# Moving q, k and x across partitions by DMA so that attention runs on 64x64 tiles: one change to a fused attention and feed-forward kernel

## The chip, the cores and the metric

The kernel runs on one core of one Trainium2 chip. The metric is the time of one execution on the device, in microseconds (us). The profiler's span of a run is about 1.8 us shorter than its time. Where not said otherwise, all quoted times are medians of fast executions; an execution is called slow when it took over 1.5 % longer than the fastest of its kernel. PE is the matrix engine (TensorE), DVE is VectorE, ACT is ScalarE, POOL is GpSimd and SP is SyncE, which here only issues DMAs.

## The reference

Attention inside chunks of 64 tokens, then a feed-forward block in which two products are multiplied:

```python
# q, k, v: (8, 8, 576, 64) = batch, heads, tokens, head dim; chunk = 64
scores = scale * np.matmul(q_c, k_c.transpose(0, 1, 2, 4, 3))
scores = scores - np.max(scores, axis=-1, keepdims=True)
attn = np.exp(scores)
attn = attn / (np.sum(attn, axis=-1, keepdims=True) + 1e-09)
out = np.matmul(attn, v_c)
# ... heads joined: x is (4608, 512)
a = x @ w1            # w1, w2: (512, 1024)
b = x @ w2
h = a * b @ w3        # w3: (1024, 1024)
return (h @ w_out).astype(np.float32)     # w_out: (1024, 512)
```

The tokens are worked off as 18 "pairs" of 256 tokens (four chunks). The kernel multiplies w3 and w_out once into one matrix `w3o`.

## The kernel before

A string gives the order in which steps are emitted, each a letter and a pair: `l` loads q, k, v; `T` transposes q and k within blocks of 32 partitions (DVE); `S` scores (PE); `E` exponentials (ACT); `P` values (PE); `N` division (DVE); `X` transposes x (DVE); `A` and `B` the products a and b in four parts (PE); `C` copies a out of PSUM (ACT); `M` multiplies it by b (DVE); `O` the output product (PE); `Y` copies it (ACT) and issues its DMA (SP). Each engine takes its steps strictly in this order. All PSUM results share one pool of four tiles of 2 x 512 f32 in each partition.

```python
ps = ctx.enter_context(tc.tile_pool(name="ps", bufs=4, space=bass.MemoryType.PSUM))

def do_T(p, s):
    if s == 0:
        qkT_t[p] = asb.tile([P, 2, 2, H, CH], bf, tag="qkT", bufs=2, name="qkT")
    inorder(nc.vector.transpose(...))          # cut

def do_S(p):                                   # 8 x 2 x 4 = 64 products, contraction over 32
    qkT = qkT_t.pop(p)
    s_t[p] = psum("s_ps")
    for h in range(H):
        for e in range(2):
            for i in range(NB):
                mm(s_t[p][half[i % 2], i // 2, h * CH:(h + 1) * CH],
                   lhsT=qkT[blk[i], 1, e, h, :],
                   rhs=qkT[blk[i], 0, e, h, :], start=(e == 0), stop=(e == 1))
# do_P: 2 x 2 x 2 x 4 x 2 = 64 products, e[half, ..., 32 columns] by vbuf[half]     (cut)

def do_C(p, j):
    a_t[p, j] = msb.tile([P, 512], f32, tag="a_sb", bufs=3, name="a_sb")
    inorder(nc.scalar.copy(a_t[p, j][:], ps_t[p, j][:, 0, :]))
# do_M: ab = a_sb * ps_t[p, j][:, 1, :], which frees the PSUM tile of A and B        (cut)

def do_Y(p):                                   # last pair: in two halves (cut)
    inorder(nc.scalar.copy(o_sb[:, u0:u1], t[:, u0:u1]))
    inorder(nc.sync.dma_start(
        out[p * PT + u0 * UT:p * PT + u1 * UT].rearrange("(u p) n -> p u n", p=UT), o_sb[:, u0:u1]))
```

The softmax here doesn't subtract the row's maximum and nothing guards it: scores larger than these inputs give would overflow.

## Time and profile before

| | |
|---|---|
| time | 262.31 us, median of 3 (262.27 to 262.46) |
| PE busy | 89 % of the span |
| mean granted PE clock | 0.986 of full speed |
| two pairs in the steady part | 24.0 us (158.1 to 182.1), two output products among them |

From the page of the kernel before: the busy time of each engine, and three rows that cut the span into 40 slices of 6.5 us (busy tenths of PE, tenths of the granted clock, and the mean busy share of the 16 DMA engines).

```profile
PE 231.9 (89%) x3796; PEld 169.8 (65%) x3808; DVE 153.7 (59%) x231; ACT 84.1 (32%) x114; POOL 84.5 (32%) x112
PE   0259948999999698999899999999999999999992
PEclk9999995999999999999999999999999999999999
DMA  7999999999999999929931004002200220220344
```

PE starts late, has some gaps while the loads come in (the DMA row stands at 7 and then at 9 for the first 17 slices, 110 us), and from then on is full to the end. DMA is nearly idle in the second half: it looks as if it could take on work for nothing.

The timeline of PE in the kernel before, a stretch of two pairs. Columns: start, length, engine, line, operation, output and inputs, tile and shapes, count; in brackets idle time before it and what ended it.

```profile
158.12 7.15 PE L88 MATMUL ab_ps<-xt,w 128*128 128x256 bf16 x64
165.20 0.70 PE L88 MATMUL pv<-vbuf,e 64*32 64x65 bf16 x64
165.83 0.71 PE L88 MATMUL s_ps<-qkT 32*64 32x64 bf16 x64
166.66 7.15 PE L88 MATMUL ab_ps<-xt,w 128*128 128x256 bf16 x64
...
175.21 7.07 PE L88 MATMUL o_ps<-w3o,ab 128*128 128x512 bf16 x31
182.11 0.27 PE L88 MATMUL ab_ps<-xt,w 128*128 128x256 bf16 x1
```

Start to start, the values (`pv`) take 0.63 us and the scores (`s_ps`) 0.83 us of every pair. No bracket stands on any of these lines: PE waits for nothing.

All DMA instructions on `out_dram` in the kernel before (nanoseconds, min/median/max), and their time from issue to landing:

```profile
L249 SPq DMA_DIRECT2D out_dram<-o_sb x19: 344/372/429, 107.0 to 256.8; - x19
DMA to landing us min/median/max: 2.0/2.8/4.7
```

SP has 19 DMAs in the whole kernel. The issue of one takes it 0.37 us.

### The profile page before, as it was taken

How to read it: one execution, taken by the hardware profiler on the slowest of the kernel's cores; microseconds unless marked ns; L12 is line 12 of the kernel's file. 1: busy time of each engine (PE TensorE's matmuls, PEld its weight loads, DVE VectorE, ACT ScalarE, POOL GpSimd, SP SyncE). 2: the span in 40 equal slices, each digit the busy share in tenths (PEclk: the TensorE clock that was granted, in tenths of full speed). 3: DMA queues.
4: the chain of work that ended last, by engine and by line, in shares of the span. 5: the costliest groups of instructions: out<-in, count | busy, mean ns of one | idle time of the engine just before them, and what ended most of it. 6: DMA issues, size and time to landing. Idle time of an engine off the chain costs nothing.

```text
span 260.2 us, 8288 instructions
## 1 busy us (share of the span) xinstructions
PE 231.9 (89%) x3796; PEld 169.8 (65%) x3808; DVE 153.7 (59%) x231; ACT 84.1 (32%) x114; POOL 84.5 (32%) x112
## 2 busy tenths in 40 slices
PE   0259948999999698999899999999999999999992
PEld 0248836875686586588568857884886588484440
DVE  1676685799989869539824982697276047121000
ACT  1112430324433243333233343432443333242331
POOL 8956854778975996105200000000000000000000
PEclk9999995999999999999999999999999999999999
DMA  7999999999999999929931004002200220220344
GB/s 78 168 196 178 179 200 196 187 170 170 171 170 173 161 173 173 196 83 93 75 103 62 3 4 161 5 3 80 84 3 3 83 83 0 77 86 27 135 164 161
DMA packets 89619, 29.38 MB, mean 113 GB/s; under 512 B 75760, under 2 KB 84976, under 8 KB 89584
## 3 DMA queue, kind: packets, MB, share of 16 engines
q0 software_dynamic: 84672, 19.41, 80.1%
...
## 4 chain that ended last, share of the span: by engine, by line
PE 65%; DMA 14%; POOL 8%; DVE 6%; issue 3%; ACT 2%; ACTq 0%; POOLq 0%
PE ab_ps L88 35%; PE o_ps L88 24%; DMA w<-in_moe_w_dram 8%; PE w_ps L88 4%; DMA wo<-in_moe_w_out_dram 4%; DVE ab L232 3%; POOL qk L91 3%; POOL vbuf L91 3%; DMA qk<-in_k_dram 2%; ACT a_sb L227 2%; POOL w L91 2%; DVE qkT L159 1%; PE pv L88 1%; PE s_ps L88 1%; POOL wo L91 1%
## 5 line engine op out<-in xcount | busy, mean ns | idle before, releaser
L88 PE MATMUL ab_ps<-xt,w 128*128 128x256 bf16 x1152 | 132.6, 277 | 3.0 <-issue 2.2
L88 PEld LDWEIGHTS <-w 128*128 128x128 bf16 x1152 | 114.0, 99 | 19.9 <-issue 2.6
L232 DVE TENSOR_TENSOR ab<-a_sb,ab_ps 128x512 bf16<-128x512 f32 x72 | 48.6, 676 | 69.5 <-ACT a_sb L227 69.5
L227 ACT COPY a_sb<-ab_ps 128x512 f32<-128x512 f32 x72 | 42.1, 585 | 92.9 <-PE ab_ps L88 87.1
L88 PE MATMUL o_ps<-w3o,ab 128*128 128x512 bf16 x280 | 62.9, 379 | 1.4 <-DVE ab L232 0.6
L88 PEld LDWEIGHTS <-ab 128*128 128x128 bf16 x288 | 28.1, 98 | 33.5 <-issue 0.6
L159 DVE STREAM_TRANSPOSE qkT<-qk 128x1024 bf16<-128x1024 bf16 x36 | 45.7, 1292 | 6.6 <-DMA qk<-in_q_dram 6.5
...
L248 ACT COPY o_sb<-o_ps 128x1024 f32<-128x1024 f32 (+1 forms) x19 | 18.3, 967 | 46.4 <-PE o_ps L88 46.4
L204 DVE STREAM_TRANSPOSE xt<-xn 128x512 bf16<-128x512 bf16 x36 | 25.5, 709 | 1.1
L200 DVE TENSOR_TENSOR xn<-pv,rc 128x512 bf16<-128x512 f32 x36 | 24.9, 691 | 1.2
L175 ACT ACTIVATE e<-s_ps 128x1024 bf16<-128x1024 f32 x18 | 18.4, 1023 | 22.1 <-PE s_ps L88 22.1
L88 PE MATMUL s_ps<-qkT 32*64 32x64 bf16 x1152 | 13.6, 198 | 11.7 <-DVE qkT L159 10.8
...
L88 PEld LDWEIGHTS <-qkT 32*64 32x64 bf16 x1152 | 11.5, 110 | 13.3 <-DVE qkT L159 10.9
L88 PE MATMUL pv<-vbuf,e 64*32 64x65 bf16 x1152 | 13.0, 201 | 7.4 <-issue 4.0
L88 PEld LDWEIGHTS <-e 64*32 64x32 bf16 x1152 | 10.1, 91 | 11.8 <-issue 7.6
L88 PE MATMUL w_ps<-wo,w3T 128*128 128x512 bf16 x60 | 14.3, 379 | 0.2
L91 POOL DMA_DIRECT2D w<-in_moe_w_dram x16 | 11.1, 694 | 6.4 <-DMA wo<-in_moe_w_out_dram 2.8
L88 PEld LDWEIGHTS <-w3T 128*128 128x128 bf16 x64 | 6.1, 98 | 6.7
L256 DVE STREAM_TRANSPOSE w3T<-w 128x1024 bf16<-128x1024 bf16 x8 | 9.6, 1213 | 0.0
(9 smaller groups left out, 15.1 us busy)
## 6 DMA issues: line engine op xcount, KB each, us to landing
...
```

The costliest lines, as they stand in the source:

```text
L88: return inorder(nc.tensor.matmul(*a, **kw))
L91: return inorder(nc.gpsimd.dma_start(dst, src))
L159: inorder(nc.vector.transpose(qkT_t[p][:, s].rearrange("p e h (y t) -> p h t e y", t=2), qk_t[p][:, s].rearrange("p h (t e y) -> p h t e y ...
L175: inorder(nc.scalar.activation(e_t[p][:].rearrange("p u h q -> p u (h q)"), s_t.pop(p)[:], Exp, scale=scale, bias=0.0))
L200: inorder(nc.vector.tensor_mul(xn_t[p, u][:], pv[:, :, :, 0:D], rc.to_broadcast([P, 2, 4, D])))
L204: inorder(nc.vector.transpose(xt[:, :, t0:t0 + UT].rearrange("p o (m y) -> p m o y", y=BL), xn_t.pop((p, u))[:].rearrange("p r (c n) (z o) ...
L227: inorder(nc.scalar.copy(a_t[p, j][:], ps_t[p, j][:, 0, :]))
L232: inorder(nc.vector.tensor_mul(ab_t[p][:, 2 * j:2 * j + 2, :].rearrange("p j t -> p (j t)"), a_t.pop((p, j))[:], ps_t.pop((p, j))[:, 1, :]))
L248: inorder(nc.scalar.copy(o_sb[:, u0:u1], t[:, u0:u1]))
L256: inorder(nc.vector.transpose(w3T_t[f][:].rearrange("p k (f y) -> p f k y", y=BL), w3[:, NB * f:NB * (f + 1), :].rearrange("p f (k x) -> p ...
```

## The change

The intent: from pair 4 on, let DMA bring the two 32-row parts of each contraction into one 64-row half of the array, so that scores and values need 32 products each on 64x64 tiles and not 64 each on 32x64 and 64x32 tiles. `G` moves q and k, `H` moves x back; each is eight DMAs of 32 partitions, SBUF to SBUF, on SP. The new layout permutes the tokens of a pair, so an output is now a DMA whose DRAM side is written `(c y) n` with c = 4. Besides, the first quarter of w1, w2 is loaded behind pair 0, the order is retuned, and the last output is cut in three. Core of the diff (the order string, renamed views and warm-up products on zeros are cut):

```diff
+    def move(dst, src):
+        inorder(nc.sync.dma_start(dst, src))
+    def do_G(p):
+        qkT = qkT_t.pop(p)
+        qkm_t[p] = asb.tile([P, 2, 2, H, CH], bf, tag="qkm", bufs=2, name="qkm")
+        for i in range(NB):
+            for e in range(2):
+                move(qkm_t[p][blk[i // 2 * 2 + e], i % 2], qkT[blk[i], e])
 ... do_S, p >= 4
+            for h in range(H):
+                for i in (0, 3, 1, 2):
+                    mm(s_t[p][half[i % 2], i // 2, h * CH:(h + 1) * CH],
+                       lhsT=qkm[half[i // 2], i % 2, 1, h, :], rhs=qkm[half[i // 2], i % 2, 0, h, :],
+                       start=True, stop=True)
 ... do_P, p >= 4
+                    for g, r in ((0, 0), (1, 1), (1, 0), (0, 1)):
+                        mm(pv[half[g], r, m * W:(m + 1) * W], lhsT=e[half[r], u, 4 * g + m, :],
+                           rhs=vbuf[p % 7][half[r], u, 4 * g + m, 0:W], start=True, stop=True)
+    def do_H(p):
+        for k_ in range(2):
+            for i in range(NB):
+                move(xt[blk[i // 2 * 2 + k_], p, i % 2], xm_t[p][blk[i], k_])
 ... outputs
+    def out_rows(p, u):
+        return out[p * PT:(p + 1) * PT].rearrange("(c u y) n -> u c y n", u=2, y=BL)[u]
+        for u in range(2):
+            move(out_rows(p, u), o_sb[:, u])
```

More of the change, by code (lines that the diff above doesn't have):

```diff
@@ L9 @@
 ORDER = """
-l0 l1 i0 i1 i2 l2 i3 l3 o h0 h1 l4 l5 T0.0 T0.1 l6 S0 E0 T1.0 P0 N0.0 T1.1 l7 X0.0 S1 N0.1 E1 X0.1
-P1 A0.0 N1.0 X1.0 N1.1 B0.0 C0.0 X1.1 A1.0 M0.0 B1.0 C1.0 A0.1 M1.0 B0.1 T2.0 C0.1 A1.1 M0.1 B1.1
-T2.1 l8 C1.1 A0.2 M1.1 B0.2 C0.2 A1.2 M0.2 B1.2 C1.2 A0.3 M1.2 B0.3 C0.3 T3.0 S2 A1.3 M0.3 E2 T3.1
-B1.3 C1.3 P2 l9 M1.3 S3 N2.0 E3 X2.0 N2.1 P3 X2.1 N3.0 A2.0 X3.0 B2.0 C2.0 N3.1 A2.1 M2.0 B2.1 X3.1
-C2.1 A2.2 M2.1 B2.2 C2.2 A2.3 M2.2 B2.3 V0 C2.3 A3.0 M2.3 B3.0 V1 C3.0 A3.1 M3.0 B3.1 V2 C3.1 A3.2
@@ L15 @@
-M3.1 B3.2 C3.2 V3 A3.3 M3.2 B3.3 C3.3 T4.0 W0 M3.3 T4.1 l10 S4 T5.0 Z0 W1 E4 V4 T5.1 V5 P4 l11 Z1 V6
-S5 W2 E5 N4.0 X4.0 N4.1 X4.1 V7 A4.0 Z2 T6.0 B4.0 C4.0 A4.1 T6.1 B4.1 C4.1 M4.0 A4.2 M4.1 B4.2 T7.0
-C4.2 P5 l12 M4.2 S6 N5.0 A4.3 E6 X5.0 B4.3 N5.1 C4.3 W3 X5.1 M4.3 T7.1 T8.0 P6 l13 Z3 T8.1 S7 A5.0
-N6.0 E7 X6.0 B5.0 C5.0 N6.1 A5.1 M5.0 B5.1 X6.1 C5.1 T9.0 A5.2 B5.2 C5.2 M5.1 T9.1 A5.3 B5.3 C5.3
-M5.2 A6.0 M5.3 B6.0 C6.0 P7 l14 M6.0 S8 N7.0 A6.1 E8 X7.0 N7.1 B6.1 C6.1 X7.1 A6.2 M6.1 B6.2 C6.2
@@ L20 @@
-T10.0 A6.3 M6.2 B6.3 C6.3 T10.1 P8 l15 S9 M6.3 N8.0 O0 E9 X8.0 N8.1 X8.1 T11.0 O1 Y0 T11.1 A7.0 Y1
-B7.0 C7.0 A7.1 M7.0 B7.1 C7.1 A7.2 M7.1 B7.2 C7.2 A7.3 M7.2 B7.3 C7.3 P9 l16 M7.3 S10 N9.0 A8.0 E10
-X9.0 N9.1 B8.0 C8.0 X9.1 A8.1 M8.0 B8.1 C8.1 T12.0 A8.2 M8.1 B8.2 C8.2 T12.1 A8.3 M8.2 B8.3 C8.3 P10
-l17 M8.3 S11 N10.0 O2 E11 X10.0 N10.1 X10.1 T13.0 O3 T13.1 Y2 A9.0 Y3 B9.0 C9.0 A9.1 M9.0 B9.1 C9.1
-A9.2 M9.1 B9.2 C9.2 A9.3 M9.2 B9.3 C9.3 P11 M9.3 S12 N11.0 A10.0 E12 X11.0 N11.1 B10.0 C10.0 X11.1
@@ L25 @@
-A10.1 M10.0 B10.1 C10.1 T14.0 A10.2 M10.1 B10.2 C10.2 T14.1 A10.3 M10.2 B10.3 C10.3 P12 M10.3 S13
-N12.0 O4 E13 X12.0 N12.1 X12.1 T15.0 O5 T15.1 Y4 A11.0 Y5 B11.0 C11.0 A11.1 M11.0 B11.1 C11.1 A11.2
-M11.1 B11.2 C11.2 A11.3 M11.2 B11.3 C11.3 P13 M11.3 S14 N13.0 A12.0 E14 X13.0 N13.1 B12.0 C12.0
-X13.1 A12.1 M12.0 B12.1 C12.1 T16.0 A12.2 M12.1 B12.2 C12.2 T16.1 A12.3 M12.2 B12.3 C12.3 P14 M12.3
-S15 N14.0 O6 E15 X14.0 N14.1 X14.1 T17.0 O7 T17.1 Y6 A13.0 Y7 B13.0 C13.0 A13.1 M13.0 B13.1 C13.1
-A13.2 M13.1 B13.2 C13.2 A13.3 M13.2 B13.3 C13.3 P15 M13.3 S16 N15.0 A14.0 E16 X15.0 N15.1 B14.0
@@ L31 @@
-C14.0 X15.1 A14.1 M14.0 B14.1 C14.1 A14.2 M14.1 B14.2 C14.2 A14.3 M14.2 B14.3 C14.3 P16 M14.3 S17
-N16.0 O8 E17 X16.0 N16.1 X16.1 O9 Y8 A15.0 Y9 B15.0 C15.0 A15.1 M15.0 B15.1 C15.1 A15.2 M15.1 B15.2
-C15.2 A15.3 M15.2 B15.3 C15.3 P17 M15.3 A16.0 N17.0 X17.0 B16.0 C16.0 N17.1 A16.1 M16.0 B16.1 C16.1
-X17.1 A16.2 M16.1 B16.2 C16.2 A16.3 M16.2 B16.3 C16.3 O10 M16.3 O11 Y10 A17.0 Y11 B17.0 C17.0 A17.1
-M17.0 B17.1 C17.1 A17.2 M17.1 B17.2 C17.2 A17.3 M17.2 B17.3 C17.3 O12 M17.3 O13 Y12 O14 Y13 O15 Y14
@@ L36 @@
-O16 Y15 O17 Y16 Y17
+l0 i0 l1 i1 i2 i3 l2 l3 o h0 h1 l4 l5 D0.0.8.64 T0.0 T0.1 l6 S0 E0 P0 D1.0.1.512 N0.0 X0.0 N0.1 X0.1
+T1.0 A0.0 T1.1 l7 B0.0 C0.0 S1 M0.0 A0.1 E1 B0.1 C0.1 P1 M0.1 A0.2 N1.0 X1.0 B0.2 C0.2 N1.1 A0.3
+X1.1 B0.3 C0.3 M0.2 A1.0 T2.0 B1.0 C1.0 M0.3 A1.1 T2.1 l8 B1.1 C1.1 M1.0 S2 M1.1 A1.2 E2 T3.0 B1.2
+C1.2 T3.1 P2 l9 A1.3 M1.2 N2.0 B1.3 C1.3 X2.0 S3 N2.1 E3 X2.1 M1.3 A2.0 B2.0 C2.0 P3 M2.0 A2.1 N3.0
+X3.0 B2.1 C2.1 N3.1 A2.2 X3.1 B2.2 C2.2 M2.1 A2.3 M2.2 B2.3 V0 C2.3 A3.0 M2.3 B3.0 V1 C3.0 A3.1 M3.0
@@ new lines @@
+B3.1 V2 C3.1 W0 M3.1 V3 T4.0 W1 V4 Z0 V5 T4.1 l10 W2 Z1 V6 G4 V7 T5.0 W3 Z2 T5.1 G5 A3.2 Z3 B3.2
+T6.0 C3.2 S4 A3.3 M3.2 E4 T6.1 B3.3 C3.3 G6 P4 l11 M3.3 S5 N4.0 E5 O0 N4.1 X4.0 X4.1 T7.0 H4 O1 Y0
+T7.1 T8.0 G7 T8.1 P5 l12 Y1 S6 N5.0 E6 O2 N5.1 G8 X5.0 X5.1 A4.0 T9.0 H5 Y2 B4.0 C4.0 T9.1 A4.1 B4.1
+M4.0 C4.1 T10.0 A4.2 B4.2 C4.2 M4.1 A4.3 T10.1 B4.3 C4.3 M4.2 A5.0 M4.3 B5.0 C5.0 P6 l13 M5.0 S7
+N6.0 E7 G9 A5.1 N6.1 B5.1 C5.1 X6.0 A5.2 X6.1 B5.2 M5.1 H6 C5.2 A5.3 M5.2 B5.3 C5.3 P7 l14 M5.3 S8
+N7.0 E8 G10 O3 N7.1 X7.0 X7.1 T11.0 H7 A6.0 Y3 T11.1 B6.0 C6.0 A6.1 M6.0 B6.1 T12.0 C6.1 A6.2 M6.1
@@ new lines @@
+B6.2 T12.1 C6.2 A6.3 M6.2 B6.3 C6.3 P8 l15 M6.3 S9 N8.0 E9 G11 A7.0 N8.1 B7.0 C7.0 X8.0 A7.1 X8.1
+B7.1 M7.0 H8 C7.1 A7.2 M7.1 B7.2 C7.2 A7.3 M7.2 B7.3 T13.0 C7.3 P9 l16 S10 M7.3 E10 G12 N9.0 O4 N9.1
+X9.0 X9.1 T13.1 H9 A8.0 Y4 B8.0 C8.0 A8.1 M8.0 B8.1 T14.0 C8.1 A8.2 M8.1 B8.2 T14.1 C8.2 A8.3 M8.2
+B8.3 C8.3 P10 l17 M8.3 S11 N10.0 E11 G13 A9.0 N10.1 B9.0 C9.0 X10.0 A9.1 X10.1 B9.1 M9.0 H10 C9.1
+A9.2 M9.1 B9.2 C9.2 A9.3 M9.2 B9.3 T15.0 C9.3 P11 S12 M9.3 E12 G14 N11.0 O5 N11.1 X11.0 X11.1 T15.1
@@ new lines @@
+H11 A10.0 Y5 B10.0 C10.0 A10.1 M10.0 B10.1 T16.0 C10.1 A10.2 M10.1 B10.2 T16.1 C10.2 A10.3 M10.2
+B10.3 C10.3 P12 M10.3 S13 E13 G15 N12.0 A11.0 N12.1 B11.0 C11.0 X12.0 A11.1 X12.1 B11.1 M11.0 H12
+C11.1 A11.2 M11.1 B11.2 C11.2 A11.3 M11.2 B11.3 T17.0 C11.3 P13 S14 M11.3 E14 G16 N13.0 O6 N13.1
+X13.0 X13.1 T17.1 H13 A12.0 Y6 B12.0 C12.0 A12.1 M12.0 B12.1 C12.1 A12.2 M12.1 B12.2 C12.2 A12.3
+M12.2 B12.3 C12.3 P14 M12.3 S15 E15 G17 N14.0 A13.0 N14.1 B13.0 C13.0 X14.0 A13.1 X14.1 B13.1 M13.0
+H14 C13.1 A13.2 M13.1 B13.2 C13.2 A13.3 M13.2 B13.3 C13.3 P15 M13.3 S16 E16 N15.0 O7 N15.1 X15.0
@@ new lines @@
+X15.1 H15 O8 Y7 A14.0 Y8 B14.0 C14.0 A14.1 M14.0 B14.1 C14.1 A14.2 M14.1 B14.2 C14.2 A14.3 M14.2
+B14.3 C14.3 P16 M14.3 S17 E17 N16.0 A15.0 N16.1 B15.0 C15.0 X16.0 A15.1 X16.1 B15.1 M15.0 H16 C15.1
+A15.2 M15.1 B15.2 C15.2 A15.3 M15.2 B15.3 C15.3 P17 M15.3 O9 N17.0 N17.1 X17.0 X17.1 H17 O10 Y9
+A16.0 Y10 B16.0 C16.0 A16.1 M16.0 B16.1 C16.1 A16.2 M16.1 B16.2 C16.2 A16.3 M16.2 B16.3 C16.3 A17.0
+M16.3 B17.0 C17.0 A17.1 M17.0 B17.1 C17.1 A17.2 M17.1 B17.2 C17.2 A17.3 M17.2 B17.3 C17.3 O11 M17.3
+O12 Y11 O13 Y12 O14 Y13 O15 Y14 O16 Y15 O17 Y16 Y17
@@ L102 @@
     w3o = wpool.tile([P, FO, DM], bf, name="w3o")
-    xt = wpool.tile([P, KO, NT], bf, name="xt")
+    xt = wpool.tile([P, NP, 2, KO, UT], bf, name="xt")
+    zero = consts.tile([P, 512], bf, name="zero")
+    inorder(nc.vector.memset(zero[:], 0.0))
     vbuf = [consts.tile([P, 2, H, VW], bf, name=f"vbuf{i}") for i in range(7)]
@@ L151 @@
     blk = [slice(i * BL, (i + 1) * BL) for i in range(NB)]
-    qkT_t, s_t, e_t, pv_t, xn_t = {}, {}, {}, {}, {}
+    qkT_t, qkm_t, s_t, e_t, pv_t, xn_t, xm_t = {}, {}, {}, {}, {}, {}, {}
+    def move(dst, src):
+        inorder(nc.sync.dma_start(dst, src))
     def do_T(p, s):
@@ L159, in do_T @@
         inorder(nc.vector.transpose(
-            qkT_t[p][:, s].rearrange("p e h (y t) -> p h t e y", t=2),
+            qkT_t[p][:, :, s].rearrange("p e h (y t) -> p h t e y", t=2),
             qk_t[p][:, s].rearrange("p h (t e y) -> p h t e y", t=2, e=2)))
-    def do_S(p):
-        qkT = qkT_t.pop(p)
-        s_t[p] = psum("s_ps")
-        for h in range(H):
-            for e in range(2):
-                for i in range(NB):
+    def do_G(p):
[4 more added lines that the diff above has]
+                move(qkm_t[p][blk[i // 2 * 2 + e], i % 2], qkT[blk[i], e])
+    def do_S(p):
+        s_t[p] = s_t.pop(p) if p in s_t else psum("s_ps")
+        if p < 4:
+            qkT = qkT_t.pop(p)
+            for h in range(H):
+                for e in range(2):
+                    for i in range(NB):
+                        mm(s_t[p][half[i % 2], i // 2, h * CH:(h + 1) * CH],
+                           lhsT=qkT[blk[i], e, 1, h, :], rhs=qkT[blk[i], e, 0, h, :],
+                           start=(e == 0), stop=(e == 1))
+        else:
+            qkm = qkm_t.pop(p)
+            for h in range(H):
+                for i in (0, 3, 1, 2):
                     mm(s_t[p][half[i % 2], i // 2, h * CH:(h + 1) * CH],
-                       lhsT=qkT[blk[i], 1, e, h, :],
-                       rhs=qkT[blk[i], 0, e, h, :], start=(e == 0), stop=(e == 1))
+                       lhsT=qkm[half[i // 2], i % 2, 1, h, :], rhs=qkm[half[i // 2], i % 2, 0, h, :],
+                       start=True, stop=True)
     def do_E(p):
@@ L177, in do_E, with do_P @@
             Exp, scale=scale, bias=0.0))
-    def do_P(p, u):
-        e = e_t[p] if u == 0 else e_t.pop(p)
-        pv = pv_t[p, u] = psum("pv")
-        for n in range(2):
-            for qh in range(2):
-                for g in range(NB):
-                    for r in range(2):
-                        at = (2 * qh + n) * W
-                        mm(pv[blk[g], r, at:at + W],
-                           lhsT=e[half[r], u, 2 * g + n, qh * BL:(qh + 1) * BL],
-                           rhs=vbuf[p % 7][half[r], u, 2 * g + n, 0:W], start=True, stop=True)
-    def do_P2(p):
-        do_P(p, 0)
-        do_P(p, 1)
+    def do_P(p):
+        e = e_t.pop(p)
+        for u in range(2):
+            pv = pv_t[p, u] = psum("pv")
+            for m in range(4):
+                if p < 4:
+                    for g in range(NB):
+                        for r in range(2):
+                            mm(pv[blk[g], r, m * W:(m + 1) * W],
+                               lhsT=e[half[r], u, 2 * g + m % 2, m // 2 * BL:(m // 2 + 1) * BL],
+                               rhs=vbuf[p % 7][half[r], u, 2 * g + m % 2, 0:W], start=True, stop=True)
+                else:
+                    for g, r in ((0, 0), (1, 1), (1, 0), (0, 1)):
+                        mm(pv[half[g], r, m * W:(m + 1) * W], lhsT=e[half[r], u, 4 * g + m, :],
+                           rhs=vbuf[p % 7][half[r], u, 4 * g + m, 0:W], start=True, stop=True)
     def do_N(p, u):
@@ L198, in do_N, with do_D @@
         inorder(nc.vector.reciprocal(rc[:], pv[:, :, :, D:W]))
-        xn_t[p, u] = asb.tile([P, 2, 4, D], bf, tag="xn", bufs=2, name="xn")
-        inorder(nc.vector.tensor_mul(xn_t[p, u][:], pv[:, :, :, 0:D], rc.to_broadcast([P, 2, 4, D])))
+        if u == 0:
+            xn_t[p] = asb.tile([P, 2, 2, 4, D], bf, tag="xn", bufs=2, name="xn")
+        inorder(nc.vector.tensor_mul(xn_t[p][:, u], pv[:, :, :, 0:D], rc.to_broadcast([P, 2, 4, D])))
     def do_X(p, u):
-        t0 = p * PT + u * UT
-        inorder(nc.vector.transpose(
-            xt[:, :, t0:t0 + UT].rearrange("p o (m y) -> p m o y", y=BL),
-            xn_t.pop((p, u))[:].rearrange("p r (c n) (z o) -> p (r c) o n z", c=2, o=KO)))
-    ab_t, ps_t, a_t = {}, {}, {}
+        if p < 4:
+            inorder(nc.vector.transpose(
+                xt[:, p, :, :, u * CH:(u + 1) * CH].rearrange("p c o (r y) -> p r c o y", y=BL),
+                xn_t[p][:, u].rearrange("p r (c n) (z o) -> p (r c) o n z", c=2, o=KO)))
+        else:
+            if u == 0:
+                xm_t[p] = asb.tile([P, 2, KO, UT], bf, tag="xm", bufs=2, name="xm")
+            inorder(nc.vector.transpose(
+                xm_t[p][:, u].rearrange("p o (c y) -> p c o y", y=BL),
+                xn_t[p][:].rearrange("p u r m d -> p (u r) m d")[:, :, 2 * u:2 * u + 2]
+                .rearrange("p c n (z o) -> p c o n z", o=KO)))
+        if u == 1:
+            xn_t.pop(p)
+    def do_H(p):
+        for k_ in range(2):
+            for i in range(NB):
+                move(xt[blk[i // 2 * 2 + k_], p, i % 2], xm_t[p][blk[i], k_])
+        xm_t.pop(p)
+    ab_t, ps_t, a_t = {}, {}, {}
+    def do_D(which, p, n, cols):
+        d, key = (s_t, p) if which == 0 else (ps_t, (p, 0))
+        if key not in d:
+            d[key] = psum("z_ps")
+        for _ in range(n):
+            mm(d[key][:, 0, 0:cols], lhsT=zero[:, 0:P], rhs=zero[:, 0:cols], start=True, stop=True)
     def mm_ab(p, j, which):
@@ L215, in mm_ab @@
                    lhsT=w[:, ki, (2 * j + i) * P:(2 * j + i + 1) * P],
-                   rhs=xt[:, ki, p * PT:(p + 1) * PT], start=(ki == 0), stop=(ki == KO - 1))
+                   rhs=xt[:, p, :, ki, :], start=(ki == 0), stop=(ki == KO - 1))
     def do_A(p, j):
-        ps_t[p, j] = psum("ab_ps")
+        ps_t[p, j] = ps_t.pop((p, j)) if (p, j) in ps_t else psum("ab_ps")
         mm_ab(p, j, 0)
@@ L234, in do_M, with mm_o, do_Y @@
             ps_t.pop((p, j))[:, 1, :]))
+    def out_rows(p, u):
+        return out[p * PT:(p + 1) * PT].rearrange("(c u y) n -> u c y n", u=2, y=BL)[u]
+    def mm_o(p, u, n0, n1):
+        for ki in range(FO):
+            mm(ps_t[p][:, u, n0:n1], lhsT=ab_t[p][:, ki, u * UT:(u + 1) * UT],
+               rhs=w3o[:, ki, n0:n1], start=(ki == 0), stop=(ki == FO - 1))
     def do_O(p):
         ps_t[p] = psum("o_ps")
-        for u in range(2):
-            for ki in range(FO):
-                mm(ps_t[p][:, u, :], lhsT=ab_t[p][:, ki, u * UT:(u + 1) * UT],
-                   rhs=w3o[:, ki, :], start=(ki == 0), stop=(ki == FO - 1))
-        del ab_t[p]
-    def do_Y(p):
-        o_sb = msb.tile([P, 2, DM], f32, tag="o_sb", name="o_sb")
-        t = ps_t.pop(p)
-        for u0, u1 in ((0, 1), (1, 2)) if p == NP - 1 else ((0, 2),):
-            inorder(nc.scalar.copy(o_sb[:, u0:u1], t[:, u0:u1]))
-            inorder(nc.sync.dma_start(
-                out[p * PT + u0 * UT:p * PT + u1 * UT].rearrange("(u p) n -> p u n", p=UT), o_sb[:, u0:u1]))
+        if p < NP - 1:
+            for u in range(2):
+                mm_o(p, u, 0, DM)
+            del ab_t[p]
+            return
+        t = ps_t[p]
+        o_sb = msb.tile([P, 2, DM], f32, tag="o_sb", name="o_sb")
+        for u, n0, n1, copy in ((0, 0, DM, nc.scalar.copy), (1, 0, DM // 2, nc.scalar.copy),
+                                (1, DM // 2, DM, nc.vector.tensor_copy)):
+            mm_o(p, u, n0, n1)
+            inorder(copy(o_sb[:, u, n0:n1], t[:, u, n0:n1]))
+            move(out_rows(p, u)[:, :, n0:n1], o_sb[:, u, n0:n1])
+    def do_Y(p):
+        if p == NP - 1:
+            return
+        o_sb = msb.tile([P, 2, DM], f32, tag="o_sb", name="o_sb")
+        inorder(nc.scalar.copy(o_sb[:], ps_t.pop(p)[:]))
+        for u in range(2):
+            move(out_rows(p, u), o_sb[:, u])
     w3T_t = {}
@@ L282, in load_half3 @@
         load_w3(i * n, (i + 1) * n)
-    do = {"l": load_pair, "i": load_w12, "o": load_wo, "h": load_half3, "T": do_T, "S": do_S, "E": do_E,
-          "P": do_P2, "N": do_N, "X": do_X, "A": do_A, "B": do_B, "C": do_C, "M": do_M, "V": do_V,
+    do = {"l": load_pair, "q": lambda p: load_qk(p, (0,)), "k": lambda p: load_qk(p, (1,)), "v": load_v, "i": load_w12, "o": load_wo, "h": load_half3, "T": do_T, "S": do_S, "E": do_E, "G": do_G, "H": do_H,
+          "P": do_P, "N": do_N, "X": do_X, "A": do_A, "B": do_B, "C": do_C, "M": do_M, "D": do_D, "V": do_V,
           "W": do_W, "Z": do_Z, "O": do_O, "Y": do_Y}
```

## The prediction

> **What bounds it now.** The page gives PE 89% busy. The timeline of PE shows three stages. (a) To about 40 us loading bounds it: PE idles 8.6 us before the first scores, then 1.1 + 2.2 + 1.1 + 0.75 us around pairs 0 and 1, and 1.1 + 3.2 us at 36-40 us waiting for pairs 2 and 3; the granted clock falls to 0.76 in 40-50 us (the windows view). (b) From 40 to 256 us PE is nearly always busy: two pairs take 24.0 us (158.1 to 182.1), namely 4 x 3.5 us of a/b products, 2 x 3.45 us of output products and 2 x (0.63 values + 0.84 scores with the change of mode). (c) The end, from the last product at 255.6 us, is 4.6 us: copy, then output DMA landing 2.1 us after issue.
>
> **What changes.**
> 1. Scores and values of pairs 4-17: 64 products each become 32. Before, 64 take 0.63 us, 9.9 ns each. If the instruction stream set that, 32 take 0.32 us; if weight loads on only four tiles set it, less is won. I take 0.42: 0.2 us x 28 = 5.5 us less PE, all on the critical path. PE also gets 1792 fewer instructions[...].
> 2. 16 moves a pair on SP. The 19 output issues took 0.37 us each, so 8 take 3 us, plus about 2 us to land: 5 us from transpose to product, 6 us of SP a pair, under the pair's 12. The order puts 8 us or more of other PE work between, so in steady state they cost nothing. During saturated loading (DMA share about 2 in 60-110 us) they may land later: 0 to 4 us of stalls around pairs 4 to 7.
> 3. The first w quarter behind pair 0: A0 can start near 14.7 us, not 17.5, and A0-A3 then run while loads arrive. The later stall at 36-40 goes, but PE then meets w3, which landed only at 45-50 us (chain of waits), and some gain is lost. Net 3-5 us.
> 4. Output goes out as two DMAs per pair, whose DRAM side has an outermost dimension of 4, not 128. The Trainium skill, DMA: Bandwidth & Descriptors, section "Why a DMA increments its semaphore by 16 and not by 1", says the engines used are the largest number up to 16 dividing both sides' slowest dimension: here 4. No output in this trace has that shape. Its packets of 2 KB took 81 ns (queue table), so four engines move 512 KB in about 5.2 us, against 3.46 us per pair on PE. Seven output stages end the kernel (O11-O17): the queue would end about 15 us after PE's pace. Mid-kernel it hides.
>
> **Sum.** 262.3 - 5.5 - 4 + 2 = 255 if outputs spread over 16 engines; about 269 if on four. The tail was tuned finely in this change (last output cut in three, two engines copying), which speaks against a 15 us queue there; I give four engines 40%. Point 257, range 250-271.
>
> **What would show it.** Step 1: 32-product groups in the PE timeline at 0.3-0.45 us, two-pair period about 23.2 us. Step 2: waits of score and a/b products for moves: short, and only before 110 us. Step 3: a/b products start near 15 us, no 3 us gap at 37. Step 4: landing of 256 KB outputs: about 2 us (16 engines) or 4 and more (four); in the last 30 us, DMA near 97 GB/s with ACT copies waiting for DMA, against 150 GB/s.
>
> **What would make it wrong.** Score groups still 0.63 us on four tiles: +5 us. Moves queueing behind loads: more stalls at pairs 4-7. The four-engine output.

## The result, and the profile after

| | before | after |
|---|---|---|
| median | 262.38 us, 4 runs (262.27 to 263.2) | 334.32 us, 4 runs (330.99 to 335.64) |
| ratio | 1 | 1.2714, 95 % interval 1.2608 to 1.282 |
| mean granted clock of the profiled run | 0.986 | 0.882 |

The result is correct. A ratio, here and below, is the mean time of one kernel's fast runs over the mean of the other's fast runs of the same rounds, so it is not quite the ratio of the medians. The change made the kernel 72 us slower.

The same rows of the page, after (slices of 8.3 us):

```profile
PE 239.8 (72%) x2915; PEld 168.7 (51%) x2929; DVE 153.8 (46%) x233; ACT 83.8 (25%) x114; POOL 84.5 (25%) x112
PE   0499799769930097497599199599999999996220
PEclk9999999978995569699599789879999999999555
DMA  9999999999999569729927333333422322122222
```

PE has 881 fewer instructions in the records but is no shorter busy. It has holes in the middle (the row's 3, 0, 0, 1), after some of which the granted clock is down at 0.5 to 0.6, and in the last four slices, 33 us, it has little to do. There the DMA row stands at 2, and stays there.

From the list of waits after (engine, line and output that waited, for what; total us, times, longest):

```profile
DVE qkT L166 <- DMA qkm<-qkT: 25.8, 4, 13.4
DVE qkT L166 <- DMA xt<-xm: 21.2, 4, 10.0
PE ab_ps L89 <- DVE qkT L166: 18.7, 1, 18.7
ACT o_sb L315 <- DMA out_dram<-o_sb: 28.6, 5, 9.7
```

The same list for SP's queue has a line with what SP itself stood for:

```profile
SPq L159 <- DMA out_dram<-o_sb: 15.4, 8, 3.4
```

The transposes `T` on DVE wait for moves; PE waits for what stands behind them on DVE; and ACT waits to copy an output because earlier outputs have not left. The worst case of the first kind, from the timelines of SP and then of PE after:

```profile
96.94 11.53 SPq L159 DMA_DIRECT2D qkm<-qkT  x8
108.57 5.12 SPq L159 DMA_DIRECT2D xt<-xm  x8
113.78 1.26 SPq L159 DMA_DIRECT2D out_dram<-o_sb  x2
```

```profile
116.71 3.57 PE L89 MATMUL ab_ps<-xt,w 128*128 128x256 bf16 x16 [18.68 <-DVE qkT L166]
120.21 0.65 PE L89 MATMUL pv<-vbuf,e 64*64 64x65 bf16 x32
120.67 0.62 PE L89 MATMUL s_ps<-qkm 64*64 64x64 bf16 x32
```

From 96.9 to 115.0 us SP works off one list of DMAs, while PE stands for 18.7 us. But SP isn't issuing all that time: of the first 11.53 us the eight issues themselves fill 4.5, and before the seventh and the eighth SP stood 3.4 and 3.2 us until an earlier output had landed. The trace shows why. The program has eight completion semaphores for the DMAs of SP, in strict turn, and each issue waits until the DMA eight issues before it, which had the same semaphore, has landed. So a move can wait for an output. How long SP is with one DMA now:

```profile
L159 SPq DMA_DIRECT2D qkm<-qkT x112: 507/589/2765, 56.9 to 238.4; - x112
L159 SPq DMA_DIRECT2D out_dram<-o_sb x37: 528/595/949, 82.5 to 322.7; - x37
```

And the end: the copies of outputs on ACT, then the DMA rows of the window from 284 to 334 us (40 slices).

```profile
296.55 1.01 ACT L315 COPY o_sb<-o_ps 128x1024 f32<-128x1024 f32 x1 [5.33 <-DMA out_dram<-o_sb]
301.96 1.01 ACT L315 COPY o_sb<-o_ps 128x1024 f32<-128x1024 f32 x1 [4.40 <-DMA out_dram<-o_sb]
```

```profile
DMA  0000223222222222222222222222222222222210
GB/s 8 0 0 11 20 51 113 100 103 100 103 102 102 64 69 92 70 69 98 84 92 88 67 93 77 72 92 79 93 75 79 88 93 99 89 90 84 102 54 0
```

These copies come 5.4 us apart, each let go by an output that lands, and DMA moves about 100 GB/s (113 in one slice). That is the picture the prediction gave for outputs on four engines.

### The profile page after: what moved, and what is told of

It reads as the page before. It is cut to its first block, busy times and chain, and to the rows that moved or that the text cites. A ratio compares the mean times of both kernels' runs of the same rounds, so it can differ in the third digit from the quotient of the medians.

```text
span 333.9 us, 6964 instructions
## 1 busy us (share of the span) xinstructions
PE 239.8 (72%) x2915; PEld 168.7 (51%) x2929; DVE 153.8 (46%) x233; ACT 83.8 (25%) x114; POOL 84.5 (25%) x112
## 4 chain that ended last, share of the span: by engine, by line
DMA 46%; PE 33%; SPq 5%; DVE 5%; issue 3%; ACT 2%; POOL 2%; DVEq 0%; ACTq 0%; POOLq 0%
PE ab_ps L89 21%; DMA out_dram<-o_sb 18%; DMA qkm<-qkT 11%; PE o_ps L89 10%; DMA w<-in_moe_w_dram 6%; SPq L159 5%; DMA qk<-in_k_dram 4%; DMA xt<-xm 3%; DMA qk<-in_q_dram 3%; DVE qkT L166 3%; ACT o_sb L315 2%; DVE ab L283 2%; POOL qk L92 1%; ACT a_sb L278 1%; PE s_ps L89 1%
## 5 line engine op out<-in xcount | busy, mean ns | idle before, releaser
L89 PE MATMUL ab_ps<-xt,w 128*128 128x256 bf16 x1136 | 134.0, 280 | 34.1 <-DVE qkT L166 18.7
L89 PE MATMUL o_ps<-w3o,ab 128*128 128x512 bf16 (+1 forms) x285 | 72.3, 410 | 28.9 <-DVE ab L283 17.4
L283 DVE TENSOR_TENSOR ab<-a_sb,ab_ps 128x512 bf16<-128x512 f32 x71 | 47.6, 672 | 71.5 <-ACT a_sb L278 71.5
L89 PEld LDWEIGHTS <-ab 128*128 128x128 bf16 x296 | 31.2, 106 | 66.5 <-issue 38.7
L315 ACT COPY o_sb<-o_ps 128x1024 f32<-128x1024 f32 x17 | 17.2, 1012 | 85.0 <-PE o_ps L89 45.8
L92 POOL DMA_DIRECT2D qk<-in_q_dram x24 | 19.0, 795 | 12.4 <-DMA vbuf<-in_v_dram 5.2
L92 POOL DMA_DIRECT2D qk<-in_k_dram x24 | 18.8, 790 | 4.7 <-DMA w<-in_moe_w_dram 2.7
L237 DVE STREAM_TRANSPOSE xm<-xn 128x512 bf16<-128x512 bf16 x28 | 18.3, 690 | 0.5
L89 PE MATMUL s_ps<-qkm 64*64 64x64 bf16 x448 | 8.1, 202 | 4.5 <-DMA qkm<-qkT 4.5
L89 PE MATMUL pv<-vbuf,e 64*64 64x65 bf16 (+1 forms) x704 | 9.3, 200 | 1.1 <-ACT e L198 1.1
L89 PEld LDWEIGHTS <-e 64*64 64x64 bf16 (+1 forms) x704 | 7.1, 104 | 5.3 <-issue 3.8
## 6 DMA issues: line engine op xcount, KB each, us to landing
w<-in_moe_w_dram POOLq DMA_DIRECT2D x16, 256.0 KB, 10.4
```

Of the source, the lines that this page charges most:

```text
L89: return inorder(nc.tensor.matmul(*a, **kw))
L92: return inorder(nc.gpsimd.dma_start(dst, src))
L237: inorder(nc.vector.transpose(xm_t[p][:, u].rearrange("p o (c y) -> p c o y", y=BL), xn_t[p][:].rearrange("p u r m d -> p (u r) m d")[:, : ...
L283: inorder(nc.vector.tensor_mul(ab_t[p][:, 2 * j:2 * j + 2, :].rearrange("p j t -> p (j t)"), a_t.pop((p, j))[:], ps_t.pop((p, j))[:, 1, :]))
L315: inorder(nc.scalar.copy(o_sb[:], ps_t.pop(p)[:]))
```

## The experiments

Eighteen further kernels ran. Where a value is "wrong", the data is permuted but amounts of work are those of the change.

### 1. Which part costs what: out16, nomoves, order_only, nomoves_out16

`out16` writes each output as 128 full rows again and undoes the permutation in the products' operand:

```diff
-                   rhs=xt[:, p, :, ki, :], ...
+                   rhs=xt[:, p, :, ki, :].rearrange("p c (m y) -> p m c y", y=BL), ...
-        return out[p * PT:(p + 1) * PT].rearrange("(c u y) n -> u c y n", u=2, y=BL)[u]
+        return out[p * PT + u * UT:p * PT + (u + 1) * UT]
```

`nomoves` keeps the outputs of the change but takes the old scores, values and x for all pairs (`p < 4` becomes `p < 18`, G and H do nothing, five `qkT` buffers, because each is now held until its scores). `nomoves_out16` does both. `order_only` is the kernel before with the order of the change (without G, H and the warm-ups) and five `qkT` buffers. All are correct.

> The changed kernel with the columns of a pair read in token order by the a/b products, so that each output DMA is 128 rows by 512 (outermost dimension 128, not 4); number of DMAs, moves and order kept, result right. Theory A (the 4-engine output is most of the 72 us, both in the tail and by holding up the moves behind it on the same queue): 262 to 280 us, tail from the last a/b product to the end about 28 us instead of 51, 256 KB outputs land in about 2 us. Theory B (issuing 16 moves a pair from SP at 0.59 us each, and their landing behind the loads, is most of it): only the tail comes back, 305 to 315 us.

> The changed kernel with all pairs on the old path (no moves, scores and values on the old tiles; five buffers for the transposed q,k, as the order runs transposes ahead), output DMAs still 4 outermost. Theory A: the tail of about 50 us stays and the output keeps costing in the middle, 285 us or more. Theory B: the moves gone, the middle runs at the old pace of 12.0 us a pair and only the tail is longer by 20 us: 275 to 285 us.

> The kernel before with the new order alone (first w quarter behind pair 0, W products earlier; no moves, no warm-up products, old tiles, old output DMA; five buffers for the transposed q,k). Both theories: not the cause of the loss. My sum put the earlier start at 3 to 5 us gained: 256 to 260 us. If the order itself loses (W and w3 waits in the middle), it is over 262.

> Neither moves nor 4-outermost outputs, all else of the change (order, warm-up products, last output cut in three). Both theories expect about the time of the new order alone, 256 to 260 us; if it is much slower, a third part of the change costs.

| kernel | median us (4 runs; before: 7) | ratio to before, 95 % |
|---|---|---|
| before, same chip | 262.15 | 1 |
| order_only | 260.67 | 0.9925 (0.9889 to 0.9961) |
| nomoves_out16 | 261.33 | 0.997 (0.9911 to 1.0028) |
| nomoves | 280.64 | 1.0704 (1.0677 to 1.0731) |
| out16 | 299.46 | 1.1432 (1.1394 to 1.1471) |
| the change | 334.32 (before: 262.38) | 1.2714 (1.2608 to 1.282) |

From nomoves_out16 up: the outputs' shape alone costs 280.6 - 261.3 = 19.3 us, the moves alone 299.5 - 261.3 = 38.1 us, both together 334.3 - 261.3 = 73.0 us, so 15.5 us come only where both are there (from the four ratios 14.4 us, give or take 3.4 by their intervals). `out16` fits neither of its two ranges. The order with the early w quarter is worth 1.5 us. In its trace the first a/b products do start at 14.56 us (before: 17.55), but they then wait for weights and for x, 2.35 us at 38 us for instance.

That the outputs run on four engines is read in two DMA views of the end, nomoves from 240 to 278 us, then nomoves_out16 from 225 to 258 us:

```profile
DMA  2222222322222222222222222222222222222200
q1 hardware_dynamic: 1846, 3.40, 25.0%
```

```profile
DMA  0000000000790059103930195009700016314980
out_dram<-o_sb SPq DMA_DIRECT2D x13, 256.0 KB, 2.1
```

The queue's packets take 25.0 % of sixteen engines' time, four of sixteen, all the way. In the other form the engines work in bursts and 256 KB land 2.1 us after issue. This is what the Trainium skill, DMA: Bandwidth & Descriptors, section "Why a DMA increments its semaphore by 16 and not by 1", states: the number of engines is the largest up to 16 that divides both sides' slowest dimension. The trace agrees.

### 2. Why the moves cost 38 us: moves64, moves128

Theory A (B1 in the expectations): SP cannot issue 16 moves a pair in the time of a pair. Rival (B2): the bytes, or the landing time of the moves, hold the kernel up. Both kernels start from out16 and move the same bytes with four DMAs of 64 partitions, or two of 128, for each set of eight (wrong):

```diff
-        for i in range(NB):
-            for e in range(2):
-                move(qkm_t[p][blk[i // 2 * 2 + e], i % 2], qkT[blk[i], e])
+        for e in range(2):
+            move(qkm_t[p][:, e], qkT[:, e])
```

> The kernel with 16-engine outputs, but each set of moves made of 4 DMAs of 64 partitions instead of 8 of 32: the same bytes, half the issues, partitions not changed, so the result is wrong on purpose. Theory B1 (SP issues at 0.59 us each: 18 a pair are 11.4 us, as long as PE's own pair, and everything in order behind them waits): SP needs about 6 us a pair, the stalls after 95 us go, 253 to 262 us. Theory B2 (the moves' bytes and landing beside the loads cost): 290 us or more.

> The same with 2 DMAs of 128 partitions per set: same bytes, a quarter of the issues; wrong on purpose. B1: at or below the run with 64 partitions, 250 to 256 us, which is also what the smaller products are worth when moves are free to issue. B2: 290 us or more.

moves64 took 272.71 us, ratio 1.0397 (1.0354 to 1.0441); moves128 took 265.98 us, ratio 1.0123 (1.0088 to 1.0158), with 262.83 for before. Half the DMAs give back 26.7 us of the 38, a quarter of them 33.5, at the same bytes. Both miss the ranges expected under B1 (253 to 262 and 250 to 256), but they are far under the 290 of B2. The bytes are not the cost; the number of DMAs is. A smaller number relieves several things at once, though: SP's time, the time until a set of moves has gone out and its buffer is free (section 3), and the turn of the eight semaphores.

The timeline of SP in out16, two pairs of it:

```profile
113.91 6.21 SPq L159 DMA_DIRECT2D qkm<-qkT  x8
120.22 5.47 SPq L159 DMA_DIRECT2D xt<-xm  x8
125.79 5.07 SPq L159 DMA_DIRECT2D qkm<-qkT  x8
130.96 5.64 SPq L159 DMA_DIRECT2D xt<-xm  x8
136.70 1.00 SPq L159 DMA_DIRECT2D out_dram<-o_sb  x2
```

Those lengths add up to 23.4 us for two pairs. PE needs 20.6 for two pairs with one output product (section 4). The median of one issue was 0.59 us. Rows of eight moves without any wait last 4.95 to 5.07 us; with those, two pairs would take SP 21.3 us (an estimate from these rows), still over PE's 20.6. So SP had become the slowest engine of the kernel, without room for a wait.

This bound is only a part of the 38 us. Against nomoves_out16 the scores of pair 7 start 19.3 us later in out16 (113.24 and 93.97 us), those of pair 11 33.1 us later and those of the last pair 38.9. Half of the loss is there before pair 7, while q, k and v are still being loaded: the q and k moves issued from 60 to 130 us took 5.9 us (median) to land, and PE stood 13.1 us before 109 us. The last six pairs add 5.9 us; an SP period of 21.3 to 23.4 us against PE's 20.6 would add 2 to 8 us over six pairs (an estimate from the numbers above).

The Trainium skill has a rule for the number of DMAs, in DMA: Bandwidth & Descriptors, section "Rules for kernel authors": coalesce small transfers, under 64 KB one pays mostly overhead. The moves here are 64 KB (q, k) and 32 KB (x), so the q and k moves stand at that size and not under it. The runs agree with the advice to coalesce (299.5 to 266.0 us); they don't test the figure.

### 3. The second loop, through the buffers: bufs3, g_only, g_only_bufs4

Theory D: `T` of a pair needs a free `qkT` buffer. It is free when the eight moves of an earlier pair have been issued and have landed. DVE works in order, so `M` waits behind `T`, and PE behind `M`. Then more buffers should help. `bufs3` is out16 with three `qkT` buffers (and three of `w3T`, for room); `g_only` is out16 with only the q and k moves, so values and x go the old way (8 moves a pair); `g_only_bufs4` is that with four buffers (and three of `w3T`). All are correct.

```diff
-            qkT_t[p] = asb.tile([P, 2, 2, H, CH], bf, tag="qkT", bufs=2, name="qkT")
+            qkT_t[p] = asb.tile([P, 2, 2, H, CH], bf, tag="qkT", bufs=4, name="qkT")
```

> The kernel with 16-engine outputs and three buffers instead of two for the transposed q,k (one fewer for the transposed w3). If the loss comes from VectorE standing in its order behind a transpose that waits for its buffer (held until the moves have read it), with SP itself having room: 265 to 280 us. If SP's stream of issues is the limit (B1): 290 to 300 us, hardly changed.

> 16-engine outputs and only the moves for q,k; values and x on the old path, result right. SP then issues 8 moves and an output in about 6 us a pair. B1: most of the stalls go, the gain of the 32-product scores (0.33 us a pair, 4.6 us in all) stays: 255 to 264 us. B2: half of the 38 us remains, about 280 us.

> The run with only the q,k moves, with four buffers for the transposed q,k instead of two (one fewer for transposed w3). Theory D (with SP not full, what costs is the loop: scores free a buffer, 8 issues of 0.6 us, landing, transposes on VectorE, with VectorE in order behind it): 262 to 270 us. If the buffers don't matter: 282 to 288 us as before.

bufs3: 297.0 us in the two fast runs (all four 295.06 to 300.84; two, the profiled one among them, slow; ratio of the fast two 1.1311, 1.1218 to 1.1404), hardly better than out16. With SP full, one more buffer doesn't help much. g_only: 285.88 us, 1.0875 (1.0816 to 1.0933), far above the 255 to 264 expected under B1 and near the 280 of B2. It has eight moves a pair like moves64, and took 13.2 us longer: so the number a pair is not all that counts. In moves64 the q and k of a pair leave in four issues and not eight, which frees their buffer sooner. g_only_bufs4: 266.52 us, 1.0169 (1.0116 to 1.0222). Once SP is half empty, two more buffers are worth 19.4 us, and the waits of `T` for moves, 14.2 us in the list of g_only, are gone from that of g_only_bufs4: here it was the buffers and not the bytes. So there are two limits: SP's number of DMAs, and, where that is relaxed, the loop through two buffers. moves64 and moves128 relieve both, so the 26.7 and 33.5 us are not to be put down to SP's time alone.

A side result of g_only, where 32 scores on 64x64 tiles follow values on 64x32 tiles (timeline of PE):

```profile
207.86 0.70 PE L89 MATMUL pv<-vbuf,e 64*32 64x65 bf16 x64
208.49 0.77 PE L89 MATMUL s_ps<-qkm 64*64 64x64 bf16 x32
209.33 5.99 PE L89 MATMUL o_ps<-w3o,ab 128*128 128x512 bf16 x27
```

These 32 scores last 0.77 us, and 0.84 to the next product, as long as 64 did before. In out16, after values on the same tiles, they last 0.46. The Trainium skill, TensorEngine Tiling (Array Packing), section "Key Properties", says that a change of tiling mode drains the array. That can be a part of it, but the numbers don't show it as the cause: in g_only the first four scores start 69, 155 and 125 ns apart and the rest go at the usual pace, while the scores of late_spread2 (section 5), which follow 128x128 products and so a change of mode too, need only 0.38 us to the next product. Which change costs what stays open.

### 4. Where the gain of the 32 products went: m128_spread, m128_spread2

moves128 has no waits of PE for moves over 0.5 us, and yet it is not faster than before. The timelines of PE in the same part of the order, order_only and then moves128:

```profile
122.82 0.70 PE L62 MATMUL pv<-vbuf,e 64*32 64x65 bf16 x64
123.45 0.71 PE L62 MATMUL s_ps<-qkT 32*64 32x64 bf16 x64
124.33 3.61 PE L62 MATMUL o_ps<-w3o,ab 128*128 128x512 bf16 x16 [0.17 <-DVE ab L206]
```

```profile
126.73 0.45 PE L89 MATMUL pv<-vbuf,e 64*64 64x65 bf16 x32
127.01 0.46 PE L89 MATMUL s_ps<-qkm 64*64 64x64 bf16 x32
128.25 3.61 PE L89 MATMUL o_ps<-w3o,ab 128*128 128x512 bf16 x16 [0.78 <-DVE ab L281]
```

From the values to the next large product it is 124.33 - 122.82 = 1.51 us there and 128.25 - 126.73 = 1.52 us here. Without the waits it is 1.34 and 0.74 us: the products are shorter by 0.60 us, and PE's wait for DVE's `M` is longer by 0.61. Two pairs take 20.58 us in order_only (115.74 to 136.32) and 20.59 in moves128 (119.66 to 140.25). The reason is the pool of four PSUM tiles. The tile that the next product wants comes free when the last a/b part is copied (ACT, 0.59 us) and multiplied (DVE, 0.65 to 0.69 us), and that chain can begin only when the products are done. It takes some 1.4 us, which 64 + 64 small products covered but for 0.17 us. The Trainium skill, TensorEngine Tiling (Array Packing), section "PSUM Bottleneck", warns of it: tiling speeds up the array but not the emptying of PSUM. Here it cost the whole gain of the steady part. (The 4.7 us by which moves128 is above nomoves_out16 arose earlier: the scores of pair 7 start 4.2 us later, those of the last pair 5.7.)

If so, moving the scores away from the values, behind the next a/b part, should let the gain through. `m128_spread` puts `S` and `E` of pairs 7 and up behind the next A, B, C; `m128_spread2` also holds `T` of a pair back until the scores of the pair three before it are emitted. (Both wrong, like moves128.) The order of one pair, schematically:

```diff
-P12 M10.3 S13 E13 G15 N12.0 A11.0 N12.1 B11.0 C11.0 X12.0 A11.1 ...
+P12 M10.3 G15 N12.0 A11.0 N12.1 B11.0 C11.0 S13 E13 X12.0 A11.1 ...
```

> The kernel with 2 moves of 128 partitions per set (wrong on purpose), with the scores and exp of pairs 7 on put behind the next a/b group, so that the values and scores are not back to back. Theory C (the PE time saved by 32 products is given back as a wait of 0.73 us per pair for the last a*b product to free a PSUM tile, since values and scores together are now shorter than that chain of copy and product): the 0.7 us waits for the a*b product go, the two-pair period falls from 20.6 to about 19.3 us, 257 to 260 us. If the waits have another source: 264 to 267 us.

> The 128-partition moves (wrong on purpose) with the scores put behind the next a/b group as in m128_spread, and now the transposes of q,k from pair 11 on put three pairs ahead of their scores instead of four, one behind each a*b product, so that VectorE is not held by the loop of buffers and moves. Theory C (saved PE time was given back as the 0.73 us wait for a PSUM tile): two-pair period near 19.3 us in the second half and 257 to 261 us. If C is wrong: the period stays at 20.5 us or more, 264 us or more.

Both missed in the total. m128_spread took 279.26 us (1.0652): later scores hold the `qkm` buffers longer, so moves, and with them the transposes on DVE, wait more (`T` for moves: 19.9 us in its list of waits against 6.5 in moves128). m128_spread2 took 268.35 us (1.0228), but in its late, undisturbed part the period fell to 19.63 us (155.39 to 175.02), and of the 0.7 us waits one of 0.22 is left there. Spreading alone could not have given that: with the old products, in order_only, one wait of 0.17 us in two pairs is all there is to win. What it lost, it lost earlier: PE waited 2.65 and 3.60 us for moves of x at 108 and 119 us.

### 5. Ways out: late, late_spread, late_spread2, h_on_act

`late` starts from out16: the moves begin at pair 11 (when loading is over), `H` goes out from POOL's queue, and `T` of pairs 8 to 12 is held back until the scores of the pair two before it are emitted. `late_spread` also separates scores from values as above. `late_spread2` holds `T` back to the scores of the pair three before and has three `qkT` buffers. `h_on_act` is bufs3 with `H` issued from ACT. All are correct. (The last two lines of this cut are of late_spread2 alone.)

```diff
-        if p < 4:
+        if p < 11:
 ... do_H
-                move(xt[blk[i // 2 * 2 + k_], p, i % 2], xm_t[p][blk[i], k_])
+                load(xt[blk[i // 2 * 2 + k_], p, i % 2], xm_t[p][blk[i], k_])    # load: issued by gpsimd
 ... do_T
-            qkT_t[p] = asb.tile([P, 2, 2, H, CH], bf, tag="qkT", bufs=2, name="qkT")
+            qkT_t[p] = asb.tile([P, 2, 2, H, CH], bf, tag="qkT", bufs=3, name="qkT")
```

> 16-engine outputs, moves only from pair 11 on, when the loads are over; the x moves are issued by GpSimd's queue, the q,k moves by SP, so 8 each a pair; transposes of q,k held back to two pairs ahead as in the kernel before. Result right. Theories B1 and D (issuing is the limit, not the moves themselves): no stalls over 1 us in the second half, about the time of the new order alone, 258 to 264 us, for the saved PE time is given back as waits of 0.7 us (C).

> The same with the scores and exp of pairs 11 on behind the next a/b group. C: 0.7 us a pair over 7 pairs is won, 4 to 6 us less than the run without it, 254 to 259 us, below both kernels. If C is wrong: the same as without it.

> The version with right result: moves from pair 11 on only, x moves issued by GpSimd's queue, scores behind the next a/b group, three buffers for the transposed q,k and its transposes three pairs ahead. C and D: 254 to 259 us, below both kernels. If the moves still stall VectorE: 262 us or more.

> 16-engine outputs, all moves of the change, three buffers for the transposed q,k, and the x moves issued from ScalarE's queue instead of SP's. B1 (SP's issue rate is the limit of the second half): SP needs 6 us a pair, the time falls from 299 to 270 to 285 us, less than all of it since ScalarE now stands 5 us a pair. If SP's rate is not the limit: 295 us or more.

late: 266.94 us in its three fast runs (one of four was slow), 1.0193 (1.0136 to 1.0249), above what was expected (its list has `T` waiting 10.4 us for scores and 5.9 for moves), and late_spread: 274.0 us, 1.0429 (1.0358 to 1.0499), a miss whose list looks like that of m128_spread (`T` for moves 15.6 us, for scores 11.9). h_on_act: 310.15 us, 1.1809 (1.1745 to 1.1873), worse than on SP: ACT itself now stood still with its copies behind the issues (64.0 us of waits of `o_sb` copies for moves of x), so it says nothing about SP's load.

late_spread2: **257.96 us** (257.18 to 259.0, 6 runs), ratio 0.9846 (0.9813 to 0.9878): faster than both kernels, by 1.5 % over before. Its PE timeline:

```profile
145.27 1.91 PE L89 MATMUL ab_ps<-xt,w 128*128 128x256 bf16 x16
147.11 0.45 PE L89 MATMUL s_ps<-qkm 64*64 64x64 bf16 x32
147.49 5.41 PE L89 MATMUL ab_ps<-xt,w 128*128 128x256 bf16 x48
152.83 0.45 PE L89 MATMUL pv<-vbuf,e 64*64 64x65 bf16 x32
153.37 1.91 PE L89 MATMUL ab_ps<-xt,w 128*128 128x256 bf16 x16
```

No bracket, that is no wait, and two pairs take 19.63 us (145.27 to 164.90) against 20.58 in order_only. That is 0.475 us a pair, and seven pairs make 3.3 us; the measured gain is 2.7 us over order_only and 3.4 over nomoves_out16, which also has the cut last output (both of another round and chip).

### 6. The 15.5 us that need both: m128_out4, out4_act, out16_act

Theory Q: the moves stand behind slow outputs in SP's queue. Theory R: each output issue got longer on an SP without room (0.60 us against 0.43 in out16; but in nomoves, with no moves at all, it is 0.54). Theory E: the outputs keep four of the DMA engines busy, on which loads and moves have their share too. `m128_out4` is moves128 with the outputs of the change (wrong); `out4_act` and `out16_act` are the change and out16 with outputs issued from ACT's queue (correct).

```diff
+    def emit(dst, src):
+        inorder(nc.scalar.dma_start(dst, src))
-            move(out_rows(p, u), o_sb[:, u])
+            emit(out_rows(p, u), o_sb[:, u])
```

> The interaction of moves and four-engine outputs is 334.3 - 261.3 - 19.3 - 38.1 = 15.5 us. Here the moves are 4 a pair (wrong values on purpose) and the outputs are the change's own, on four engines. moves128 with 16-engine outputs took 266.0, and the outputs alone cost 19.3 us. Theory Q (moves stand behind slow outputs in SP's queue and for its landing slots): a stall of moves behind outputs is still there with few issues, but there are fewer moves, so 288 to 296 us, with waits of DVE or PE for moves of several us. Theory R (each output issue is longer, 0.60 for 0.43 us, on an SP that has no room left): SP has room here, so only the sum, 285 us (283 to 287).

> The change with its four-engine outputs issued from ScalarE's queue instead of SP's; the moves stay on SP. Read against out16_act, which has the outputs on 16 engines: theory Q says the outputs no longer hold up the moves, so the two differ by the outputs alone, 19 us (17 to 22), and this one takes 305 to 320 us. If the outputs slow the moves because they share the four engines themselves and not the queue (theory E), the difference stays near 35 us, as between the change (334.3) and its 16-engine form (299.5).

> The 16-engine form of the change with outputs issued from ScalarE's queue. SP loses 35 issues of about 0.43 us, 15 us of 108 us filled; if SP's issue time is what holds the moves' loop, this gains up to 8 us over 299.5: 290 to 299 us; ScalarE pays 0.4 to 0.6 us an issue, 1 us per pair, which it has room for (25 % busy).

| outputs on | 16 engines | 4 engines | difference | last scores start, 16 and 4 engines |
|---|---|---|---|---|
| no moves | 261.33 | 280.64 | 19.3 | 199.0, 200.9 |
| 4 moves a pair | 265.98 | 295.74 | 29.8 | 204.5, 217.1 |
| 16 moves a pair | 299.46 | 334.32 | 34.9 | 237.7, 253.8 |
| 16 moves, outputs from ACT | 300.0 | 343.76 | 43.8 | 237.0, 261.6 |

(The last column is from the profiled runs. Two of the four runs of out16_act were slow; 300.0 is of the fast two.) R falls: with four moves a pair SP has room, and most of the extra cost is still there. The queue alone isn't it either: with the outputs on another queue the difference does not shrink to 19 but grows. But Q doesn't fall with that. The eight semaphores are shared by SP and ACT, so in out4_act too the moves waited for outputs: SP stood 27.6 us for outputs to land (10 times, at most 9.5) against 5.3 in out16_act, and in the change 15.4 against 2.7 in out16. m128_out4 lies in the range that Q gave, 288 to 296. out16_act, relieved of 37 output issues on SP, gained nothing in the total: from the scores of pair 7 to the last it was 3.8 us quicker than out16 (120.3 against 124.2 us), but it came to them 3.2 us later.

The last column shows where the extra cost sits. Four-engine outputs delay the last scores by only 1.9 us without moves, but by 12.6, 16.1 and 24.6 us with them; so it arises before the end of the kernel. In m128_out4 12.4 of the 12.6 us are there at the scores of pair 7, and the period after 120 us is as in moves128, 20.58 us (140.85 to 161.43): it arises while loading is on. In the change 7.4 of the 16.1 us are there at pair 7, and the rest comes later. There, in its PE timeline:

```profile
100.14 3.57 PE L89 MATMUL ab_ps<-xt,w 128*128 128x256 bf16 x16 [8.70 <-DMA xt<-xm]
106.59 0.43 PE L89 MATMUL pv<-vbuf,e 64*64 64x65 bf16 x16 [2.87 <-DVE ab L281]
110.01 0.43 PE L89 MATMUL pv<-vbuf,e 64*64 64x65 bf16 x16 [2.98 <-DVE ab L281]
```

and a `T` waited 11.4 us for a load of q. The loads of 256 KB of k issued from 60 to 130 us landed after 13.6 us (median), against 10.8 in moves128. The chain of work that ended last goes through one load of k that took 29.5 us (78.5 to 108.1; the one at that place in moves128 took 18.8), and SP stood only 0.8 us for outputs. That fits E. In the change the chain goes, from 83.4 to 108.0 us, through two outputs that took 11.6 and 11.7 us to land, and then through the moves that waited for them. That fits Q in the form of the shared semaphores. No run had more semaphores, or gave the four engines to one kind of traffic alone, so both are read from traces, their shares are not known, and the cause of the 15.5 us is not shown.

## Why the prediction was wrong, point by point

- **Step 2 failed: "6 us of SP a pair, under the pair's 12", "in steady state they cost nothing".** Three terms were mis-sized. An issue was taken at 0.37 us, from the outputs; for moves it measured 0.59, and 16 of them with outputs took SP 11.7 us a pair, small waits included (23.4 for two). The pair is 10.3 us in the new order with one output product for two pairs, not 12. Occupancy above the period means a bound, not something hidden. And the stalls while loading were put at "0 to 4 us" around pairs 4 to 7, with moves that land in about 2 us; in out16 the scores of pair 7 came 19.3 us late, and q and k moves took 5.9 us to land. Moves alone cost 38 us (299.5 against 261.3), and halving their number gave 26.7 of it back. The loop through two `qkT` buffers and the in-order DVE was not seen at all: 19.4 us in g_only.
- **Step 1 failed at "all on the critical path".** The products became shorter by more than predicted (0.28 us start to start for the values in moves128, 0.42 predicted), yet the period stayed at 20.59 against 20.58 us, because the chain that frees a PSUM tile came into view. With scores and values apart the gain appears: 19.63 us.
- **Step 3 was right in its mechanism, mis-sized in its net.** Products start at 14.56 us (predicted 14.7) and wait for weights later; the net was 1.5 us (order_only) and not 3 to 5.
- **Step 4 was right as a mechanism, with a chance too low.** Four engines, about 100 GB/s, copies waiting for DMA, 19.3 us for the outputs alone against 15 predicted. The tuned-looking end was no evidence against it. "Mid-kernel it hides" held without moves (1.9 us at the last scores) and failed with them: 15.5 us more, of which the cause stays open (section 6).
- **The sum.** The prediction added small independent terms. Measured: 261.3 without both parts, + 38.1 moves (the gain of step 1 is inside it), + 19.3 outputs, + 15.5 for both together = 334.2 us.

## What to carry to other kernels

Before you replace matrix work by many small DMAs, add up the issuing engine's time per period, with the issue time of that very kind of DMA, and compare it with the period; then trace which buffer each DMA frees, who stands behind it on an in-order engine, and which earlier DMA each issue has to wait for. When you shorten small products between large ones, ask what they were hiding, here the emptying of PSUM; spread them out first. And look at the slowest dimension of both sides of every DMA that a new layout creates.

## What the Trainium skill lacked or had wrong

- DMA: Bandwidth & Descriptors, section "Issuing engines are not separate DMA queues": it says that the time to initiate a DMA is usually small relative to the DMA itself. Here one issue on SP took 0.59 us (median of 112), against 1.9 us from issue to landing (median of the x moves in out16); 16 a pair made SP the slowest engine (23.4 us for two pairs, PE 20.6), and at the same bytes a quarter of the DMAs gave 266.0 instead of 299.5 us. No page tells the time of an issue by kind of DMA, which would have changed this prediction: 0.37 us for the old outputs, 0.37 to 0.43 for 128 full rows (without and with moves), 0.59 for moves of 32 partitions, 0.54 to 0.60 for outputs on four engines (medians).
- The same page, section "Why a DMA increments its semaphore by 16 and not by 1": the rule for the number of engines held (25.0 % of 16 engines). No page gives a size for what such a DMA costs the others: 15.5 us on top of 38.1 and 19.3 us in this kernel, not removed by issuing from another queue (43.8 us between the two output forms).
- TensorEngine Tiling (Array Packing), section "PSUM Bottleneck": right, but without a size. Here a chain of about 1.4 us, ACT's copy and DVE's product, took back all of the 0.60 us a pair. None of the pages used gives such a size, or says that short products can be spread out to cover such a chain (20.58 to 19.63 us for two pairs).
